# Two 64x128 transposes for four 64x64 ones, in a fused retention and MoE kernel

## The chip, the cores and the metric

The kernel runs on one core of a Trainium2 chip, in one launch. The metric is the device time of that launch in microseconds (us). The profile is one more execution, recorded by the hardware profiler; its span runs from the core's first instruction to its last.

TensorE (PE in the profile) multiplies and transposes, VectorE (DVE), ScalarE (ACT) and GpSimd (POOL) do the elementwise work, and SyncE (SP) issues most of the DMAs. A TensorE operation is two instructions: a weight load (PEld), which puts one operand into the array, and a matmul, which streams the other one through it. A transpose is such a pair, with the data as the loaded operand and an identity matrix as the streamed one. Each pair names a part of the array, a tile, by its rows and columns: 128x128 is the whole array, four 64x64 tiles can work side by side, and so can two tiles of 64 rows by 128 columns.

## The reference

A decaying, causal, unnormalised attention over 8 batches, 8 heads, 576 positions and a head size of 64 is followed by a feed-forward block on 4608 tokens with 512 features and 1024 hidden units:

```python
scores = scale * np.matmul(q, k.transpose(0, 1, 3, 2))
Dmat   = np.where(rel >= 0, gamma[:, None, None] ** rel[None, :, :], 0.0)
attn   = np.matmul(scores * Dmat[None], v)             # -> x, 4608 x 512
h      = x @ w_in
solu   = h * softmax(h)
ln     = (solu - mean(solu)) / sqrt(var(solu) + 1e-06) * g_ln
out    = ln @ w_out
```

All inputs and the output are float32.

## The kernel before

The sequences are cut into windows of 256 positions, with the four 64-position ends of four sequences put together as one more window. That makes 18 windows; each is worked as two *steps* `i` of four heads (36 steps) and gives two *tiles* `t` of 128 tokens to the feed-forward block (36 tiles). Within a step the heads go in two pairs, `hp` 0 and 1.

Per step, TensorE does these operations; the letters are those of the hand-written order in `ORDER["PE"]`:

- `T{i}` transposes the scaled q and k into a PSUM bank pair (`qk_tp`). For steps 0 to 11 it does so with whole-height transposes (line 360, tiles of 128x64), from step 12 on (`NQ = 12`) by the helper `turn` (line 307). ACT then copies the result out (`qe`, line 372).
- `J{i}` and `I{i}` multiply by the carried state (line 378). Between them, `Z{i}` is an empty instruction on SP (POOL for the first nine steps) that waits for `J{i}` and releases `I{i}`.
- `V{i}` (scores by v) and `K{i}` (the new state) are on line 378 too, `S{i}` (the scores) on line 422. All five use 64x64 tiles.

Per tile it does `M1_t` (line 502, 8 matmuls of 128x128 by 512 columns, x by w_in), `L{t}`, the transposes of the normalised hidden units (`ln_tp`: line 571, 128x128, for tiles 0 to 7; from tile 8 on, `NL = 8`, by `turn` on line 307), and `M2_t` (line 598, 8 matmuls by w_out). ACT copies `L`'s result out (`le`, line 582).

`turn(dst, src, odd)` transposes a block of 128 rows by 128 columns in quarters. `r` is the half of the rows and also the PSUM bank of the result; `e` is the half of the columns, which becomes the half of the partitions. With `odd` set (head pair `hp = 1`) the two halves of the partitions change places, which is the swap of the two heads. One call makes four transposes on the four 64x64 tiles. `T` calls it eight times, four times with `odd` and four times without, in the order q pair 0, q pair 1, k pair 0, k pair 1, two calls each. `L` calls it eight times, never with `odd`.

The order on each engine is written out in `ORDER`. A typical stretch on TensorE is

```python
"V20 K21 S21 M1_18 M2_16 L17 J21 T23 I21 V21 K22 S22 M1_19 M2_17 J22 L18 T24 I22 V22 K23 S23 "
```

A planner (`order_ops`) gives each operation a start time from `DUR` and from the instruction counts `COUNT`, with which it models how TensorE's instructions are fetched. These times interleave the engines' lists in the emitted program; within an engine the list is kept as it is. They also decide how many filler matmuls (`stir`, line 773) go into gaps before 31 us.

Of the kernel before, what the change touches and what calls it, by code (L numbers as in the profile page):

```python
# [16 lines left out]
    T=0.26, L=0.26, Tf=0.47, Lf=0.47, M1=1.73, M1a=1.3, M1b=0.44, M2=1.73, M2h=0.88, J=0.08, I=0.08, Z=0.05, S=0.23, V=0.225, K=0.13, G=0.1, WM=1.0, WS=0.95,  # L17
# [3 lines left out]
    ld=0.5, ld4=2.6, ldw=0.6, out=1.1, out4=2.2, outh=2.2, outz=1.1, lm=0.5,  # L21
)
MOVE = dict(ld=0.91, ld4=0.91, ldw=1.3, out=1.1, out4=1.1, outh=0.6, outz=0.6, lm=0.4)
COUNT = dict(T=64, L=64, Tf=32, Lf=16, S=32, V=32, K=32, J=8, I=8, G=2, WM=8, WS=2, M1a=12, M1b=4)
FETCH = ((20, 6.6), (45, 5.6), (999, 4.8))
PE_OUT = 0.2
SWITCH = 0.1
# [95 lines left out]
def order_ops(ops, caps):  # L123
# [27 lines left out]
    while len(start) < len(ops):  # L151
# [19 lines left out]
        if o.eng == "PE":  # L171
# [4 lines left out]
            mode = m  # L176
            fetched += COUNT.get(o.kind, 16)
            while fetched > ring:
# [52 lines left out]
def kernel(  # L231
# [10 lines left out]
    nc = tc.nc  # L242
    B, H, S, D = q.shape
# [28 lines left out]
    ident = const.tile([P, P], F16)  # L272
# [29 lines left out]
    ee = [slice(0, 64), slice(64, 128)]  # L302

    def turn(dst, src, odd=0):
        for r in range(2):
            for e in range(2):
                nc.tensor.transpose(  # L307
                    out=dst[ee[e ^ odd], r], in_=src[ee[r], e], identity=ident[ee[r], ee[r]]
                )

    def half(n):
        return ps["b"].rearrange("p r x -> p (r x)").bitcast(F16).rearrange(
            "p (r n q) -> p r n q", r=2, q=64)[:, :, 8 * n : 8 * n + 8]
# [33 lines left out]
    def flat(n):  # L347
        return ps["b"][:, n].bitcast(F16).rearrange("p (n q) -> p n q", q=P)

    def qk_tp(i):  # L350
        d = st[i]
        for n, src in enumerate((d["q16"], d["k16"])):
            for hp in range(2):
                for j in range(2):
                    x, pair = 4 * n + 2 * hp + j, src[:, j, 2 * hp : 2 * hp + 2]
                    if i >= NQ:
                        turn(half(0)[:, :, x], pair, hp)
                        continue
                    for e in range(2):
                        nc.tensor.transpose(out=flat(0)[ee[e ^ hp], x], in_=pair[:, e], identity=ident)  # L360
# [205 lines left out]
    def ln_tp(t):  # L566
        d = tk[t]
        for c in range(8):
            x = d["solu"][:, c * P : (c + 1) * P]
            if t < NL:  # L570
                nc.tensor.transpose(out=flat(1)[:, c], in_=x, identity=ident)  # L571
            else:
                turn(half(1)[:, :, c], x.rearrange("p (e q) -> p e q", e=2))

    def ln_ev(t):
        d = tk[t]
# [127 lines left out]
    for t in range(NT):  # L704
        w, c = divmod(t, 2)
# [15 lines left out]
        if c:  # L721
            op(f"q2{w}", "ACT", "q2", [f"ex{t}"], lambda w=w: squares(w))
            op(f"rs{w}", "POOL", "rs", [stat[t - 1], stat[t], f"q2{w}"], lambda w=w: rstd(w), [("sml", [f"oe{t}", f"oe{NT}" if t == NT - 1 else ""])])
        lb = "b"
        op(f"L{t}", "PE", "Lf" if t < NL else "L", [f"so{t}"], lambda t=t: ln_tp(t), [(x, [f"le{t}"]) for x in ("b2" if t < NL else "b1", "b3")], lb)
        op(f"le{t}", "ACT", "le", [f"L{t}"], lambda t=t: ln_ev(t), [("lnT", [f"M2_{t}", f"M2_{NT}" if t == NT - 1 else ""])], lb)
        for n in (t,) if t < NT - 1 else (t, NT):
# [9 lines left out]
    for c in range(4):  # L737
# [5 lines left out]
        out=masks, in_=nc.inline_tensor(masks_np, name="masks").ap().rearrange("p (m j) -> p m j", m=2)))  # L743
# [85 lines left out]
```

## Time and profile before

| | us |
|---|---|
| median of 3 runs | 223.62 |
| lowest and highest run | 223.28, 223.90 |
| the profiled execution's own time | 222.45 |
| its span | 220.7 |

| engine | busy us | share of the span |
|---|---|---|
| PE | 203.2 | 92% |
| PEld | 110.9 | 50% |
| DVE | 142.2 | 64% |
| ACT | 155.4 | 70% |
| POOL | 131.7 | 60% |

The mean granted TensorE clock was 0.988 of full speed. The profile's records give each matmul's start; its end is modelled, so neighbouring matmuls overlap in it and a "busy" PE says little. What a matmul costs is read from start to start. `turn` is first used at 66.0 us (`T12`) and last at 211.8 us (`L35`), with 1664 transposes: 896 from the hidden units, 384 from q and 384 from k.

### The profile page before, as it was taken

How to read it: one execution, taken by the hardware profiler on the slowest of the kernel's cores; microseconds unless marked ns; L12 is line 12 of the kernel's file. 1: busy time of each engine (PE TensorE's matmuls, PEld its weight loads, DVE VectorE, ACT ScalarE, POOL GpSimd, SP SyncE). 2: the span in 40 equal slices, each digit the busy share in tenths (PEclk: the TensorE clock that was granted, in tenths of full speed). 3: DMA queues.
4: the chain of work that ended last, by engine and by line, in shares of the span. 5: the costliest groups of instructions: out<-in, count | busy, mean ns of one | idle time of the engine just before them, and what ended most of it. 6: DMA issues, size and time to landing. Idle time of an engine off the chain costs nothing.

```text
span 220.7 us, 10333 instructions
## 1 busy us (share of the span) xinstructions
PE 203.2 (92%) x4468; PEld 110.9 (50%) x4468; DVE 142.2 (64%) x263; ACT 155.4 (70%) x303; POOL 131.7 (60%) x204
## 2 busy tenths in 40 slices
PE   7868988799999999999999999989999999999970
PEld 2434444564555555555555655545555555544440
DVE  1555579999659554765768586867667676566500
ACT  2356455478668786779697979777778878767950
POOL 2473719999886346597396967767697856001110
PEclk9996999999999999999999999999999999999998
DMA  6999999990796464779976766786863640261243
GB/s 180 304 353 341 345 323 287 279 291 19 210 266 160 113 156 106 215 222 289 324 215 205 223 200 195 228 253 176 246 189 88 146 120 6 51 147 38 61 111 83
DMA packets 65838, 42.83 MB, mean 194 GB/s; under 512 B 4088, under 2 KB 59776, under 8 KB 65792
## 3 DMA queue, kind: packets, MB, share of 16 engines
q1 hardware_dynamic: 65392, 42.02, 67.9%
q8 instruction: 35, 0.57, 1.2%
q10 hardware_dynamic: 400, 0.14, 0.3%
q14 instruction: 11, 0.09, 0.1%
HBM read 32.71 MB, written 9.44 MB: 191 GB/s over the span
## 4 chain that ended last, share of the span: by engine, by line
PE 71%; SPq 7%; DMA 7%; ACT 4%; DVE 3%; POOL 3%; issue 2%; POOLq 0%; DVEq 0%; ACTq 0%
PE score L598 25%; PE psh L502 25%; PE psx L378 7%; PE psb L307 6%; DMA qr<-in_q_dram 5%; SPq L321 3%; PE score L422 3%; DMA out_dram<-o_sb 2%; SPq L328 2%; DVE w2c L647 2%; SPq L620 1%; ACT o_sb L608 1%; PE psb L360 1%; PE psb L571 1%; PE psb L638 1%
## 5 line engine op out<-in xcount | busy, mean ns | idle before, releaser
L502 PE MATMUL psh<-w_in,xT 128*128 128x512 f16 x280 | 66.6, 380 | 2.3 <-DVE solu L534 1.5
L598 PE MATMUL score<-w2c,lnT 128*128 128x512 f16 (+1 forms) x288 | 66.6, 376 | 0.0
L520 ACT ACTIVATE e_sb<-psh 128x1024 f32<-128x1024 f32 x35 | 35.8, 1023 | 22.1 <-PE psh L502 22.0
L454 DVE TENSOR_TENSOR ret<-score,masks 128x512 f16<-128x512 f32 x72 | 46.2, 683 | 5.9 <-PE score L422 5.9
L598 PEld LDWEIGHTS <-lnT 128*128 128x128 f16 x296 | 28.6, 98 | 33.5 <-ACT lnT L582 1.0
L336 POOL TENSOR_TENSOR k<-kr,small 128x512 f16<-128x512 f32 x36 | 38.3, 1067 | 6.9 <-DMA kr<-in_k_dram 6.0
L502 PEld LDWEIGHTS <-xT 128*128 128x128 f16 x288 | 25.6, 98 | 31.4 <-issue 3.1
L336 POOL TENSOR_TENSOR q<-qr,small 128x512 f16<-128x512 f32 x34 | 36.2, 1068 | 7.9 <-DMA qr<-in_q_dram 7.9
L608 ACT ACTIVATE o_sb<-score,rs 128x512 f32<-128x512 f32 (+1 forms) x36 | 24.5, 681 | 14.6 <-PE score L598 6.8
L534 DVE TENSOR_TENSOR solu<-psh,e_sb 128x1024 f16<-128x1024 f32 x17 | 20.8, 1223 | 19.6 <-ACT e_sb L520 19.5
L480 POOL TENSOR_TENSOR g<-tt,small 128x128 f32<-128x128 f32 x32 | 13.3, 416 | 31.4 <-DVE tt L476 31.3
L529 DVE SCALAR_TENSOR_TENSOR solu<-psh,e_sb 128x1024 f16<-128x1024 f32 x18 | 22.0, 1224 | 9.2 <-ACT e_sb L520 9.2
L540 DVE BATCH_NORM_STATS2 bs<-solu 128x6 f32<-128x512 f16 x36 | 22.9, 679 | 0.1
L492 ACT CAST xT<-psx 128x512 f16<-128x512 f32 x36 | 21.2, 588 | 2.0 <-DVE g L471 1.3
L563 POOL TENSOR_TENSOR w<-q,mv 128x2 f32<-128x2 f32 x18 | 3.5, 195 | 29.8 <-ACT junk L549 16.9
L549 ACT ACTIVATE junk<-solu,s 128x1024 f16<-128x1024 f16 x18 | 20.7, 1149 | 0.6
L378 PE MATMUL psx<-qkT,s 64*64 64x128 f16 (+1 forms) x256 | 17.9, 228 | 2.3 <-SPq L410 1.3
L344 POOL CAST v<-vr 128x512 f16<-128x512 f32 x30 | 19.2, 641 | 0.0
L422 PE MATMUL score<-qkT 64*64 64x128 f16 x576 | 15.6, 221 | 2.4 <-ACT qkT L366 2.3
L582 ACT COPY lnT<-psb 128x512 f32<-128x512 f32 x28 | 16.4, 584 | 1.5 <-PE psb L307 0.8
L378 PEld LDWEIGHTS <-s 64*64 64x64 f16 x256 | 8.7, 105 | 14.6 <-issue 6.4
L378 PE MATMUL psx<-ret,v 64*64 64x128 f16 x576 | 15.9, 221 | 0.0
(64 smaller groups left out, 252.2 us busy)
## 6 DMA issues: line engine op xcount, KB each, us to landing
kr<-in_k_dram SPq DMA_DIRECT2D x32, 256.0 KB, 5.2
qr<-in_q_dram SPq DMA_DIRECT2D x32, 256.0 KB, 4.5
vr<-in_v_dram SPq DMA_DIRECT2D x32, 256.0 KB, 4.5
out_dram<-o_sb SPq DMA_DIRECT2D x64, 128.0 KB, 3.4
w_in_f<-in_moe_w_in_dram SPq DMA_DIRECT2D x4, 512.0 KB, 7.3
w_f<-in_moe_w_out_dram SPq DMA_DIRECT2D x4, 512.0 KB, 5.7
kr<-in_k_dram SPq DMA_DIRECT2D x16, 64.0 KB, 3.6
vr<-in_v_dram SPq DMA_DIRECT2D x16, 64.0 KB, 3.3
```

The costliest lines, as they stand in the source:

```text
L336: eng.tensor_tensor(out=t.rearrange("p j h d -> p h j d"), in0=st[i][nm + "r"], in1=g_of(i, base), op=ALU.mult,)
L378: m = nc.tensor.matmul(start=(c, e) not in begun, stop=False, skip_group_check=True, **kw)
L422: nc.tensor.matmul(out=sv[e][ee[c], hp, j], lhsT=qkT[ee[e], c, 1, hp, j], rhs=qkT[ee[e], c, 0, hp], start=True, stop=True,)
L454: nc.vector.tensor_tensor(out=d["ret"][:, e].rearrange("p h j q -> p h (j q)"), in0=score[e].rearrange("p (h x) -> p h x", h=2), in1=masks ...
L492: nc.scalar.copy(out=d["xT"].rearrange("p c h q -> p c (h q)"), in_=ps["x"][:, :, 0:256])
L502: nc.tensor.matmul(out=h_ps[:, half_], lhsT=st[2 * w + dc // 2]["xT"][:, c, dc % 2], rhs=w_in16[:, dc, 512 * half_ : 512 * half_ + 512], s ...
L520: nc.scalar.activation(out=d["e"], in_=hh(t), func=ACT.Exp, accum_out=ws[w]["se"][:, c : c + 1])
L529: nc.vector.scalar_tensor_tensor(out=d["solu"], in0=hh(t), scalar=1.0, in1=d["e"], op0=ALU.mult, op1=ALU.mult, accum_out=d["s1"][:, 0:1],)
L534: nc.vector.tensor_tensor(out=d["solu"], in0=hh(t), in1=d["e"], op=ALU.mult)
L540: nc.vector.bn_stats(out=bs[:, x], in_=tk[t]["solu"][:, x * 512 : x * 512 + 512])
L598: nc.tensor.matmul(out=o[:, cols], lhsT=tk[t]["lnT"][:, c].rearrange("p r q -> p (r q)"), rhs=w2c16[:, c, cols], start=(c == 0), stop=(c = ...
L608: nc.scalar.activation(out=d["osb"][:, cols], in_=o[:, cols], func=ACT.Copy, scale=ws[t // 2]["rs"][:, t % 2 : t % 2 + 1],)
```

## The change

Where there is no swap of heads, `turn` makes one transpose for each half of the rows: 64 rows by 128 columns go to all 128 partitions of the half's PSUM bank. With the swap it works as before. The planner's counts follow.

```diff
-COUNT = dict(T=64, L=64, Tf=32, Lf=16, ...
+COUNT = dict(T=48, L=32, Tf=32, Lf=16, ...
...
     def turn(dst, src, odd=0):
         for r in range(2):
+            if not odd:
+                nc.tensor.transpose(out=dst[:, r], in_=src[ee[r]], identity=ident[ee[r], ee[r]])
+                continue
             for e in range(2):
                 nc.tensor.transpose(
-                    out=dst[ee[e ^ odd], r], in_=src[ee[r], e], identity=ident[ee[r], ee[r]]
+                    out=dst[ee[1 - e], r], in_=src[ee[r], e], identity=ident[ee[r], ee[r]]
                 )
...
-                turn(half(1)[:, :, c], x.rearrange("p (e q) -> p e q", e=2))
+                turn(half(1)[:, :, c], x)
```

All of `L8` to `L35` and half of each of `T12` to `T35` change. The order of operations on every engine stays the same; on PE, 1280 transposes of 64x64 become 640 of 64x128.

More of the change, by code (lines that the diff above doesn't have):

```diff
@@ L23 @@
 MOVE = dict(ld=0.91, ld4=0.91, ldw=1.3, out=1.1, out4=1.1, outh=0.6, outz=0.6, lm=0.4)
-COUNT = dict(T=64, L=64, Tf=32, Lf=16, S=32, V=32, K=32, J=8, I=8, G=2, WM=8, WS=2, M1a=12, M1b=4)
+COUNT = dict(T=48, L=32, Tf=32, Lf=16, S=32, V=32, K=32, J=8, I=8, G=2, WM=8, WS=2, M1a=12, M1b=4)
 FETCH = ((20, 6.6), (45, 5.6), (999, 4.8))
```

## Prediction

> **What bounds the kernel now.** I read the page's engine shares and chain first.
>
> ```profile
> PE 203.2 (92%) x4468; PEld 110.9 (50%) x4468; DVE 142.2 (64%) x263; ACT 155.4 (70%) x303; POOL 131.7 (60%) x204
> PE 71%; SPq 7%; DMA 7%; ACT 4%; DVE 3%; POOL 3%; issue 2%; POOLq 0%; DVEq 0%; ACTq 0%
> ```
>
> TensorE carries 71% of the chain. As its busy time uses modelled ends, I then took the timeline of PE over one step (columns: start, length, engine, line, operation, tile rows*columns, streamed size, count):
>
> ```profile
> 122.30 1.90 PE L502 MATMUL psh<-w_in,xT 128*128 128x512 f16 x8
> 124.03 1.89 PE L598 MATMUL score<-w2c,lnT 128*128 128x512 f16 x8
> 125.85 0.45 PE L307 MATMUL psb<-ident,solu 64*64 64x64 f16 x32
> 126.13 0.23 PE L378 MATMUL psx<-qkT,s 64*64 64x128 f16 x4
> 126.19 0.29 PE L307 MATMUL psb<-ident,q 64*64 64x64 f16 x16
> 126.31 0.30 PE L307 MATMUL psb<-ident,k 64*64 64x64 f16 x16
> 126.47 0.25 PE L378 MATMUL psx<-qkT,s 64*64 64x128 f16 x4
> 126.55 0.39 PE L378 MATMUL psx<-ret,v 64*64 64x128 f16 x16
> 126.77 0.29 PE L378 MATMUL psx<-v,k 64*64 64x64 f16 x16
> 126.89 0.40 PE L422 MATMUL score<-qkT 64*64 64x128 f16 x16
> 127.22 0.39 PE L502 MATMUL psh<-w_in,xT 128*128 128x512 f16 x1
> ```
>
> From start to start, M1 takes 1.73 us, which is 8 times 0.216, and M2 starts with no gap. M2's eight would then end at 125.76, but L starts at 125.85: 0.09 us are lost where the tile goes from 128x128 to 64x64. Between L, J, T, I, V, K and S the line changes and the tile doesn't, and the single records put the usual gap there at 0 to 6 ns. From 66 to 206 us the starts leave only seven gaps over 0.3 us, 3.8 us together; the rest is a row of matmuls and these changes of tile. So in the stretch where `turn` is used, TensorE sets the pace, and ACT, the next, is busy 8.4 of 10 us there (the table by stage, 114 to 124 us).
>
> The question is then what a change of tile costs where only the rows or only the columns change. The early, whole-height T shows both (timeline, two windows):
>
> ```profile
> 46.66 0.25 PE L378 MATMUL psx<-qkT,s 64*64 64x128 f16 x4
> 46.84 0.41 PE L360 MATMUL psb<-ident,q 128*64 128x128 f16 x8
> 47.09 0.39 PE L360 MATMUL psb<-ident,k 128*64 128x128 f16 x8
> 47.41 0.25 PE L378 MATMUL psx<-qkT,s 64*64 64x128 f16 x4
> ...
> 49.22 0.41 PE L360 MATMUL psb<-ident,k 128*64 128x128 f16 x8 [0.15 <-POOL k L336]
> 49.57 0.62 PE L571 MATMUL psb<-ident,solu 128*128 128x128 f16 x8
> ```
>
> A group of concurrent matmuls with 128 columns streamed paces at 0.056 us (16 of `ret,v` on four tiles: 126.55 to 126.77). J's four from 46.66 should end at 46.72; T starts at 46.84, 0.12 late. T's k, four pairs from 47.09, should end at 47.31; the next starts at 47.41, 0.10 late. So a change of rows alone costs like a full one. In the second window only the columns change: k after a wait, from 49.22, takes four pairs of 0.056 and 0.02 more at its start and should end at 49.47; L starts at 49.57, 0.10 late. Taken from the single records, all changes without a visible wait lose 93 to 124 ns, and the second group after one comes another 10 ns (into 128x128) or 20 to 24 ns late (into 64x64 and 128x64).
>
> **The change part by part.**
>
> *Streaming.* 320 groups of four 64x64 transposes become 320 pairs of 64x128. A group now takes 31.5 ns (L: 8 groups in 0.28 us, less 0.02 for the first). A pair streams the same 64 columns, so half of the 56 ns for 128 columns, 28 ns, is the floor. Its weight load has 128 columns for 64. Loads by form:
>
> ```profile
> L598 PEld LDWEIGHTS <-lnT 128*128 128x128 f16 x296 | 28.6, 98 | 33.5 <-ACT lnT L582 1.0
> L307 PEld LDWEIGHTS <-solu 64*64 64x64 f16 x896 | 9.9, 108 | 5.1 <-issue 4.7 <-DVE bs L540 0.4
> ```
>
> A 128-column load is no longer than a 64-column one (98 against 108 ns), but no row has it on half the rows. Ends: 28 ns (320 x -3.5 = -1.1 us) and 56 ns, the pace of the 128x128 transposes of line 571, should the load of 128 columns set it (320 x 24.5 = +7.8). I take 30 ns, near the load row: -0.5 us.
>
> *Changes of tile.* `turn` without `odd` now stands on 64x128 between operations on 64x64. T runs q pair 0 (64x128), q pair 1 (64x64), k pair 0, k pair 1: three changes inside each of 24 T, 72. The others come where L and T begin and end. Counted along TensorE's order in the two programs there are 118 changes before and 231 after: 113 more, of which 48 lead into 64x64 and 65 into 64x128. Into 64x64 a change costs 93 + 22 = 0.116 us by the rows: 48 x 0.116 = 5.6. Into 64x128 the nearest rows are those that leave 64x64 with one dimension grown (64x64 to 128x64, 100 to 124 ns, plus 24) and that go to 128 columns (99 plus 10): I take 0.12, and 65 x 0.12 = 7.8. Together +13.4 us. Ends: 113 x 0.093 = 10.5 and 113 x 0.142 = 16.0; the pair 64x64 and 64x128 itself stands in no row, so that it costs nothing stays open as a rival. Queued behind each of these are V, K, S, M1 and M2 of the same step, so the loss goes straight to the next step; ACT and DVE, who wait for T and L, have slack.
>
> The Trainium skill (TensorEngine Tiling (Array Packing), Key Properties) says that a change of tiling mode drains TensorE, and a change of tile within a mode does not. The rows agree for each pair of shapes they hold. By the rule all 113 drain; without it for this pair the sum would be that of the first rival.
>
> *Fewer instructions.* 640 loads and 640 matmuls go. The Trainium skill (TensorE: Matmul & The Clock Gate, "Wait — 56ns, not 53.3ns?") has matmul starts never closer than some 25 ns; by that 640 fewer would save an estimated 16 us. The rows speak against it: 32 transposes of L start within 0.28 us, under 9 ns apart. So the saving is that of the streaming term.
>
> *Stalls that go.* Of the 3.8 us of gaps, four (0.37, 0.71, 0.58, 0.36) are I waiting for Z on SP, which stands behind DMA issues:
>
> ```profile
> 162.62 0.11 PEld L378 LDWEIGHTS <-s 64*64 64x64 f16 x4 [0.63 <-SPq L410]
> ```
>
> T lies between J and I; with some 0.4 us more in it, and SP's work unchanged while the step grows, I take 1.6 of these 2.0 us as covered. Two more (0.95 in M1 at 147 us, 0.53 in T at 106 us) show no releaser but "issue"; instructions arrive by DMA (the page's instruction queue: 35 packets, 0.57 MB, so 16 KB each), and with a seventh fewer I take 0.8 of 1.5 us as gone. Sum -2.4; ends 0 and -3.5. What comes next late is TensorE itself.
>
> Early work (up to 66 us) is untouched: T0 to T11 and L0 to L7 use other lines. Loads are issued ahead and only wait longer for buffers.
>
> *Sum:* +13.4 - 0.5 - 2.4 = +10.5 us. The profiled execution took 222.45 us (span 220.7 and 1.75 around it), which gives 232.95; it lies 1.2 under the median of the runs, so against 223.62 I forecast 234.1 us. All low ends: 10.5 - 1.1 - 3.5 = +5.9, 229.5 us. High ends without slow loads: 16.0 - 0.5 + 0 = +15.5, 239.1.
>
> **The rivals.**
>
> *Half-row tiles don't drain among themselves (faster).* If 64x64 and 64x128 count as one shape, the 113 changes cost nothing. Then -0.5 to -1.1 of streaming and about -0.8 of issue gaps remain: 222.0 us. This decides when a change between the two costs below some 12 ns (1.3 / 113). For it: both split the rows in the same way, and no row shows the pair. Against it: a change of columns alone cost 0.10 us, three times out of three.
>
> *Slow loads.* If a load of 128 columns on 64 rows sets the pace, pairs take 56 ns: +7.8 instead of -0.5, so 242.4 us. For it: no load on half the rows with 128 columns is in the trace. Against: the 98 ns row.
>
> *The drains are partly hidden.* If they cost half, because the next load may go to the other half of the rows early, or because other stalls shrink more, then about +13.4 / 2 - 0.5 - 2.4 = +3.8: 227.4 us. Against: from 64x64 tiles, where the same could happen, rows show the full price.
>
> **How the numbers follow.** Full drains with quick loads 0.70 (229.5 to 239.1, likeliest 234.1); slow loads 0.16; partly hidden 0.07; no drain 0.06; no visible change 0.01. The likeliest gives 234.1. Leaving out no drain, most of the partly hidden case and the upper part of slow loads, the range is 229.0 to 242.5. About 0.3% (0.7 us) is what a measurement of this kernel can tell from no change. Faster by more: 0.06; within: 0.02; slower: 0.92.
>
> **What would show it.** In the profile after, T's four parts should start some 0.17 to 0.19 us apart (two pairs or groups and a change) where q and k now take 0.12 each, so that T takes 0.65 to 0.75 us in place of 0.28; J should start about 0.12 us later after L; a step of 4.92 us should become 5.4 to 5.5. L's 16 transposes should start some 15 ns apart; at 28 ns the loads are slow. The SP waits of I should be mostly gone. I am wrong if T's parts follow one another without a gap, if the steps stay below 5.1 us, or if the step grows and the end doesn't.

## The result and the profile after

| | before | after |
|---|---|---|
| median us | 223.76 (4 runs) | 230.31 (4 runs, 228.82 to 231.2) |
| ratio, 95% interval | | 1.0293 [1.0223, 1.0363] |
| the profiled execution, its span | 222.45, 220.7 | 230.1, 228.3 |

The changed kernel is 2.9% slower, some 6.5 us. One of the four runs of before (228.05 us) was in a slower state; the ratio is taken without it. The page of the changed kernel, engine shares and chain by engine:

```profile
PE 213.6 (94%) x3828; PEld 116.1 (51%) x3828; DVE 142.1 (62%) x263; ACT 155.3 (68%) x303; POOL 131.4 (58%) x204
PE 80%; SPq 5%; ACT 4%; DMA 3%; DVE 2%; POOL 1%; issue 1%; POOLq 0%; DVEq 0%; ACTq 0%
```

There are 640 matmuls fewer, and TensorE has 80% of the chain in place of 71%; the other engines do what they did. One step on the timeline of PE (columns as before; line 307 is now the 64x128 transpose of `turn` and line 310 its 64x64 one, and the numbers below them are three higher):

```profile
150.19 1.89 PE L601 MATMUL score<-w2c,lnT 128*128 128x512 f16 x8
152.01 0.41 PE L307 MATMUL psb<-ident,solu 64*128 64x64 f16 x16
152.35 0.25 PE L381 MATMUL psx<-qkT,s 64*64 64x128 f16 x4
152.53 0.23 PE L307 MATMUL psb<-ident,q 64*128 64x64 f16 x4
152.69 0.26 PE L310 MATMUL psb<-ident,q 64*64 64x64 f16 x8
152.88 0.23 PE L307 MATMUL psb<-ident,k 64*128 64x64 f16 x4
153.04 0.26 PE L310 MATMUL psb<-ident,k 64*64 64x64 f16 x8
153.13 0.23 PE L381 MATMUL psx<-qkT,s 64*64 64x128 f16 x4
153.19 0.39 PE L381 MATMUL psx<-ret,v 64*64 64x128 f16 x16
153.41 0.29 PE L381 MATMUL psx<-v,k 64*64 64x64 f16 x16
153.53 0.40 PE L425 MATMUL score<-qkT 64*64 64x128 f16 x16
153.86 1.90 PE L505 MATMUL psh<-w_in,xT 128*128 128x512 f16 x8
```

T's four parts start 0.16 to 0.19 us apart, though each streams only two groups (0.06 us). T takes 0.60 us, from 152.53 to 153.13, where it took 0.28. J comes 0.34 us after L's start and not 0.28, although L's 16 transposes are as quick as its 32 were: by the single records they start 14.7 ns apart, a pair every 29.3 ns. The loads are no longer:

```profile
L307 PEld LDWEIGHTS <-solu 64*128 64x128 f16 x448 | 8.1, 95 | 6.0 <-issue 4.7 <-DVE bs L543 0.4
L310 PEld LDWEIGHTS <-q 64*64 64x64 f16 x192 | 3.5, 104 | 1.2
```

128 columns on half the rows take 95 ns, 64 columns 104. The Trainium skill (TensorE: Matmul & The Clock Gate, "Weight-path perf modes — Fast Weight Load (FWL) and DoubleRow") has loads of exactly 128 columns that are not FP32 go by a faster path; the two rows agree with that.

To see where the time went, I sorted each start-to-start interval of TensorE, from T12's first transpose to the end, in one profiled execution of each kernel. The pace of a group (31.5 ns for four 64x64 with 64 columns, 29.2 for a pair, 56 for 128 columns, 216 for 512) counts as streaming. What the first group after a change of tile comes late (to 130 ns) and the next one (to 26 ns) counts as changes; lateness over 140 ns elsewhere, or over those limits, counts as stalls. What is left is small lateness. The time after the start of the last matmul is the tail.

| us | before | after | difference |
|---|---|---|---|
| changes of tile (65, then 177 in this stretch) | 7.27 | 20.11 | +12.84 |
| transposes of `turn`, streaming | 13.04 | 12.36 | -0.68 |
| all other streaming and small lateness | 123.36 | 121.49 | -1.87 |
| stalls | 4.88 | 1.31 | -3.57 |
| after the last matmul's start (tail) | 6.07 | 5.26 | -0.81 |
| sum, from T12 on | 154.62 | 160.53 | +5.91 |
| ahead of T12 | 66.04 | 67.79 | +1.75 |

The last row isn't the change: nothing differs there, and over the eleven profiles that this document has, T12 starts anywhere from 66.0 to 68.7 us. The profile of before happens to be an early one.

### The profile page after: what moved, and what is told of

Read it like the earlier page. It is cut to its first block, busy times and chain, and to the rows that moved or that the text cites. A ratio compares the mean times of both kernels' runs of the same rounds, so it can differ in the third digit from the quotient of the medians.

```text
span 228.3 us, 9053 instructions
## 1 busy us (share of the span) xinstructions
PE 213.6 (94%) x3828; PEld 116.1 (51%) x3828; DVE 142.1 (62%) x263; ACT 155.3 (68%) x303; POOL 131.4 (58%) x204
## 4 chain that ended last, share of the span: by engine, by line
PE 80%; SPq 5%; ACT 4%; DMA 3%; DVE 2%; POOL 1%; issue 1%; POOLq 0%; DVEq 0%; ACTq 0%
PE psh L505 27%; PE score L601 26%; PE psx L381 8%; PE psb L307 7%; PE psb L310 4%; SPq L324 3%; PE score L425 3%; DMA qr<-in_q_dram 3%; PE psb L574 2%; PE psb L363 2%; DVE w2c L650 2%; SPq L331 1%; ACT qkT L369 1%; PE psb L641 1%; PE psx L505 1%
## 5 line engine op out<-in xcount | busy, mean ns | idle before, releaser
L457 DVE TENSOR_TENSOR ret<-score,masks 128x512 f16<-128x512 f32 x72 | 46.2, 682 | 7.6 <-PE score L425 7.6
L474 DVE TENSOR_TENSOR g<-psx,g 128x128 f32<-128x128 f32 x16 | 4.6, 290 | 17.4 <-PE psx L381 17.4
```

The source lines that it names most:

```text
L457: nc.vector.tensor_tensor(out=d["ret"][:, e].rearrange("p h j q -> p h (j q)"), in0=score[e].rearrange("p (h x) -> p h x", h=2), in1=masks ...
```

## The experiments

The theory after the result: a change of tile idles TensorE for 0.115 us, whichever dimension changes, and the sum of them, less what TensorE had been waiting for anyway, is the loss. The rivals: the 64x128 transposes themselves are slow; added work in T costs more than its length; the loss goes with the number of wide transposes.

### Spare transposes in the kernel before

```diff
+    def wide(dst, src):
+        for r in range(2):
+            nc.tensor.transpose(out=dst[:, r], in_=src[ee[r]], identity=ident[ee[r], ee[r]])
...
                     if i >= NQ:
+                        if j == 0 and (n, hp) == (1, 0):
+                            wide(half(0)[:, :, x], pair)
                         turn(half(0)[:, :, x], pair, hp)
```

The second cut is in `qk_tp`, which makes T. One spare 64x128 call for each T: 

> The kernel before, with one more call in each of T12 to T35: before k's first call, the same block is transposed once as two 64x128 pairs (its result is then written again by the 64x64 ones). 48 changes of tile and 24 pairs more, nothing else moved. Theory (each change of tile idles TensorE for about 0.115 us, and TensorE sets the pace): 24 x (0.114 + 0.116 + 0.03) = 6.2 us more TensorE time, of which up to 3.8 us of stalls may give back: 226.5 to 229.8 us. Rival (the changes are free, the wide transposes themselves or their loads are slow): 24 pairs at 0.056 us, +1.3 us or less: 224 to 225 us.

Measured: 227.01 us, ratio 1.0132 [1.0076, 1.0188]. The timeline of PE shows the one call (line 313 is `wide`, line 384 was 378):

```profile
151.36 0.29 PE L307 MATMUL psb<-ident,q 64*64 64x64 f16 x16
151.59 0.20 PE L313 MATMUL psb<-ident,k 64*128 64x64 f16 x2
151.72 0.32 PE L307 MATMUL psb<-ident,k 64*64 64x64 f16 x16
151.87 0.23 PE L384 MATMUL psx<-qkT,s 64*64 64x128 f16 x4
```

k starts 0.36 us after q, where it started 0.12 after it, for two transposes put in. By the accounting the changes cost 5.60 us more, 0.117 each, and the stretch from T12 on grew by 3.32. Of the 6.3 us put in (0.7 of it streaming) 3.0 came back: 1.1 of small lateness, 0.4 of stalls and 1.45 of the tail.

The same call as four 64x64 transposes (against that run):

```diff
                         if j == 0 and (n, hp) == (1, 0):
-                            wide(half(0)[:, :, x], pair)
+                            turn(half(0)[:, :, x], pair)
```

> The control of the run with a spare 64x128 call: the same spare call in the same place of T12 to T35, but as four 64x64 transposes, so no change of tile is added. Theory: 24 x 0.0315 = 0.8 us of TensorE, 223.5 to 224.8 us. Rival (any added work there costs like the wide call): 226.5 us or more.

Measured: 223.84 us against 223.65, ratio 1.0012 [0.9966, 1.0059]. The same work in the same place without a change of tile is not seen in the time. This pair separates the change of tile from the work.

Three spare 64x128 calls, ahead of every part of T but the first (against the run with one):

```diff
-                        if j == 0 and (n, hp) == (1, 0):
+                        if j == 0 and (n, hp) != (0, 0):
                             wide(half(0)[:, :, x], pair)
```

> The kernel before, with three spare 64x128 calls in each of T12 to T35 (before q pair 1, k pair 0 and k pair 1): 144 changes of tile more. Theory: 72 x 0.26 = 18.7 us more TensorE time; the stalls can be given back only once, so from one spare call to three the time should grow by the full 48 x 0.26 = 12.5 us: 238 to 242.5 us. Rival (the time that goes back grows with the added time, because much of TensorE's time is cover for something else): less than 10 us above the run with one spare call.

Measured: 238.23 us, ratio 1.0621 [1.054, 1.0703], 11.2 above one call. The changes cost 16.54 us more than before, 0.115 each, so the price is the same with 48, 112 (the change itself) and 144 more of them. Of the 12.3 us between one call and three (10.9 of changes, 1.4 of streaming) 2.4 came back as stalls: the expectation had assumed that one call would take all stalls away, and it had not.

### Half of the change

Here `turn` takes a fourth argument, and makes the 64x128 transposes only where it is 1. L alone on 64x128 (against the changed kernel):

```diff
-COUNT = dict(T=48, L=32,
+COUNT = dict(T=64, L=32,
...
-                        turn(half(0)[:, :, x], pair, hp)
+                        turn(half(0)[:, :, x], pair, hp, 0)
```

> Only L uses the 64x128 transposes, T stays on 64x64 (in the kernel before's order of operations): 158 changes of tile against 118, 40 more, 896 fewer instructions. Theory (changes of tile): 12 x 0.116 + 28 x 0.12 = 4.8 us more, 0.8 us less streaming, 1 to 3.5 us of stalls given back: 224.5 to 227 us. Rival (L, with 448 of the 640 wide transposes, brings most of the loss, because the wide transposes are slow): 228 us or more.

Measured: 223.64 us, ratio 1.0 [0.9958, 1.0041], below the theory's range. 448 of the 640 wide transposes cost nothing visible. The 40 changes cost 4.51 us, and all came back: streaming -0.46, other -1.14, stalls -1.93 and the tail -1.32. The tail's share is partly scatter: the 6.07 us in the profile of before is the longest of all, and the others have 4.6 to 5.4.

T alone on 64x128 (against the changed kernel too):

```diff
-COUNT = dict(T=48, L=32,
+COUNT = dict(T=48, L=64,
...
-                turn(half(1)[:, :, c], x)
+                turn(half(1)[:, :, c], x.rearrange("p (e q) -> p e q", e=2), 0, 0)
```

> Only T uses the 64x128 transposes, L stays on 64x64: 213 changes of tile, 95 more, though only 192 of the 640 wide transposes are in it. Theory: 47 x 0.116 + 48 x 0.114 = 10.9 us more, 0.4 less streaming, 2 to 3.5 of stalls given back: 230 to 232.5 us, no better than the whole change. Rival (loss by the number of wide transposes): 226 us or less.

Measured: 227.95 us, ratio 1.0193 [1.0132, 1.0254]. Below the range again, but 4.3 us above L alone, with 192 wide transposes against 448 and 95 changes against 40. The loss goes with the number of changes, not with that of wide transposes. The theory's error is once more the part that comes back: changes +10.73, stalls -2.72, other -1.28.

### The same transposes in another order

```diff
-        for n, src in enumerate((d["q16"], d["k16"])):
-            for hp in range(2):
+        for hp in range(2):
+            for n, src in enumerate((d["q16"], d["k16"])):
                 for j in range(2):
```

In the changed kernel this puts the 64x128 parts of q and k side by side: 

> The changed kernel with T's parts in the order q pair 0, k pair 0, q pair 1, k pair 1: the same transposes, but one change of tile inside T and not three, 48 changes fewer (183 in the program). Theory: 48 x 0.115 = 5.5 us less TensorE time than the changed kernel, of which 0.5 to 2 us may come back as stalls: 225 to 227 us. Rival (the wide transposes or their loads cost the time): no change against the changed kernel, 229 to 231 us.

Measured: 224.81 us, ratio to before 1.0024 [0.998, 1.0067]. By the medians, swapping two loops takes back some 5.5 us of the 6.5, with all 640 wide transposes in place:

```profile
149.74 0.23 PE L307 MATMUL psb<-ident,q 64*128 64x64 f16 x4
149.81 0.22 PE L307 MATMUL psb<-ident,k 64*128 64x64 f16 x4
149.96 0.26 PE L310 MATMUL psb<-ident,q 64*64 64x64 f16 x8
150.04 0.23 PE L310 MATMUL psb<-ident,k 64*64 64x64 f16 x8
150.11 0.23 PE L381 MATMUL psx<-qkT,s 64*64 64x128 f16 x4
```

q and k of one shape start 0.07 to 0.08 us apart, and only the step between the shapes takes 0.15. This kernel still has 64 changes more than before from T12 on (129 and 65), yet its stretch from T12 to the end is only 0.81 us longer (155.43 and 154.62 us): what came back covers nearly all of them.

One step further, T is split in two operations, U (pair 0 of q and k) and T (pair 1), and the order is rewritten (one step as an example):

```diff
-        "L17 J21 T23 I21 V21 K22 S22 M1_19 M2_17 J22 L18 T24 I22 "
+        "L17 U23 J21 T23 I21 V21 K22 S22 M1_19 M2_17 L18 U24 J22 T24 I22 "
```

> The changed kernel with the 64x128 work of a step in one piece: L, then q pair 0 and k pair 0, then J, then q pair 1 and k pair 1, then I (where L can go first). 152 changes of tile, 34 more than before, 32 of them into 64x128, and all 1280 instructions fewer. Theory: 32 x 0.11 + 2 x 0.116 = 3.7 us more than before, 0.7 less streaming, 1.5 to 2.5 less by gaps in which instructions are late, 0 to 3 us more of I waiting for Z, since only half of T lies between J and I now: 223.5 to 227 us. Rival (loss by wide transposes, not by changes): as the changed kernel, 229 to 231 us.

Measured: 225.06 us, ratio 1.0064 [1.0024, 1.0103]. Changes were +3.39 us only, but stalls rose to 5.90 from 4.88: with half of T between J and I, I waits for Z in nearly every step, and most of these stalls are some 0.15 us each. What the order saved in changes it paid in an exposed wait.

L alone on 64x128 and moved to stand right behind M1 or M2 (against the run with L alone):

```diff
-        "M1_19 M2_17 J22 L18 T24 I22 V22 "
+        "M1_19 M2_17 L18 J22 T24 I22 V22 "
```

> Only L on 64x128, T on 64x64, and L moved to stand right behind M1 or M2 in each step, so that it takes one change more and not two: 143 changes, 25 more than before, 896 fewer instructions. Theory: 28 x 0.105 - 3 x 0.116 = 2.6 us more, 0.8 less streaming, 1 to 2 less by gaps in which instructions are late; L may wait for VectorE, which it reaches earlier: 222.5 to 225.5 us, level with the kernel before. Rival (L's earlier place exposes VectorE's product in each step, 0.2 us or more): 227 us or more.

Measured: 224.04 us, ratio 1.0017 [0.9982, 1.0053]: changes +2.29, stalls +0.21. It is level with L alone in the old order: that one has 15 more changes (2.2 us) and 2.1 us less of stalls, five of its gaps and eight here being I waiting for Z. None of these versions beats the kernel before.

### What the gaps without a releaser come from

In the profile of before, TensorE's waits from 69 to 208 us, then those of the run with a spare 64x64 call (columns: who waited for whom, us, times, longest):

```profile
PE psx L378 <- SPq L410: 1.3, 4, 0.5
PE psh L502 <- issue: 0.8, 1, 0.8
PE psb L307 <- issue: 0.3, 1, 0.3
```
```profile
PE psh L504 <- issue: 1.1, 1, 1.1
PE psx L380 <- SPq L412: 1.1, 2, 0.9
PE score L424 <- issue: 0.9, 1, 0.9
```

"Issue" gaps without any semaphore appear in four programs: before, both one-call runs and three calls, which have 8936 TensorE instructions or more. The change and its variants, with 7656 to 8552, have none. One such gap lies in the middle of M1, between its second matmul and its third (timeline of PE in before):

```profile
146.87 0.60 PE L502 MATMUL psh<-w_in,xT 128*128 128x512 f16 x2
148.26 0.38 PE L502 MATMUL psh<-w_in,xT 128*128 128x512 f16 x1 [0.79 <-issue]
```

So the changed kernel was given its number of instructions back, each wide pair being made twice:

```diff
-        for r in range(2):
+        for r in (0, 1) if odd else (0, 1, 0, 1):
             if not odd:
```

> The changed kernel with each 64x128 pair of transposes made twice in a row: as many TensorE instructions as in the kernel before again, the 231 changes of tile of the changed kernel, and 320 pairs more. Streaming: 320 x 0.0293 = 9.4 us. Theory one (the gaps of TensorE without a releaser, 1 to 2.4 us in the programs with 8900 instructions or more and none in those with up to 8500, come with the number of instructions): they are back, 1 to 2.4 us in one to three gaps, and the time is 240.5 to 242.5 us. Theory two (they went because the steps grew longer, or with the shape of the transposes): no such gap, 239 to 240 us.

Measured: 238.44 us, ratio 1.0693 [1.0597, 1.0789], and no such gap: the number alone isn't it, and the time lies below both ranges, 8.1 us above the change for 9.3 of streaming. What sorts the programs is how fast they use instructions up. Over the steps from 100 to 185 us, TensorE's records (weight loads and matmuls) per us are

| before, spare 64x64 | one spare call | three | twice | T alone | L alone, L first | grouped, joined | after |
|---|---|---|---|---|---|---|---|
| 52.6 | 51.3 | 49.0 | 47.1 | 46.8 | 46.2, 45.8 | 42.4 to 42.5 | 41.0 |
| gaps | gaps | one gap | none | none | none | none | none |

The first three columns have gaps (1.06 to 2.4 us in all), the others none.

The traces show more. Number TensorE's loads and matmuls in the order of their starts. All seven "issue" gaps between 69 and 210 us end at number 190 or some multiple of 256 beyond it, and each program has as many 16 KB packets in its instruction queue (35 in before, 30 in the changed kernel) as it has such places. Pair the second place with the first packet, the third with the second, and so on: in all eleven traces no place is passed less than 1.37 us after its packet landed. The instruction behind each of the seven gaps starts 1.37 to 1.53 us after the landing, and in the seven programs without gaps every place between 69 and 210 us has at least 1.67 us. By this the gaps are waits for the next block of 256 instructions. That a program falls behind because it uses instructions up too fast fits the table, but no run changed the rate by itself.

## Why the prediction was right or wrong

The direction and the mechanism held, and the time, 230.31, lies in the range, but only 1.3 us inside its low end. The forecast of +10.5 us was 4 too high. Point by point:

- *Changes of tile*: +13.4 forecast, +12.84 measured, 0.115 each (93 + 22 ns in the forecast is 0.115 too, not 0.116, which is 0.05 us in its sum). The pair that no row of before held costs 93 to 95 ns plus 20 to 24 into 64x64, and from 64x64 into 64x128 102 to 128 plus 9 to 11. The rival in which half-row tiles don't drain among themselves is out, and with it the partly hidden drains. The rule of the Trainium skill (TensorEngine Tiling (Array Packing), Key Properties) holds for this pair too.
- *Streaming*: 30 ns a pair forecast, 29.3 measured; -0.5 against -0.68. The slow loads are out (95 ns).
- *Stalls that go*: this term was mis-sized. I counted the gaps over 0.3 us, 3.8, and let 2.4 go; 3.57 went, nearly all. Of the gaps of I waiting for Z some 1.8 went (1.6 forecast), of the two issue gaps all 1.5 (0.8 forecast), and 0.3 ahead of S that had no place in the sum. Beside them 1.87 us went that I had not counted at all: lateness of a few ns to 0.1 us each, mostly within T's and L's 64x64 groups and on both sides of I. In the kernel before, each of q's groups behind the first comes 5 ns late on the mean, in the changed kernel none does. It isn't the new shape alone that does this: with one or three spare wide calls, where all 64x64 groups stay, the small lateness falls by some 1.1 to 1.2 us as well, and with the spare 64x64 call by 0.1. Together 5.4 us came back and not 2.4.
- *The sum*: 12.84 - 0.68 - 5.44 - 0.81 (the tail, whose scatter I had not allowed for) = 5.91 us from T12 on, in place of 13.4 - 0.5 - 2.4 = 10.5. The runs' 6.5 us are 0.6 more; one profile of each kernel can't say where these lie.
- *What would show it*: T's parts 0.16 to 0.19 us apart (0.17 to 0.19 forecast), T 0.60 (0.65 to 0.75), J some 0.06 later (0.12), a step of 5.30 us here (M1 at 153.86 and again at 159.16) and 5.40 at the median of those from 100 to 185 us (5.4 to 5.5). All as expected or a little under.

## What to carry to other kernels

Where TensorE sets the pace, count the places where the tile's shape changes along its order, not the instructions: here each cost 0.115 us of TensorE's time, as much as some 15 of the 64x64 transposes. When a shape is worth having for part of the work, put that work side by side; swapping two loops was worth some 5.5 us. And when time is added to an engine, read all of its lateness first, the small intervals too, because the new time fills it before it shows at the end: L alone put in 4.5 us of changes and its time stayed that of the kernel before.

## What was not expected of the hardware

The price of a change of tile doesn't depend on how much changes: only the columns (64x128 and 64x64), only the rows (64x64 and 128x64) and both (64x64 and 128x128) all lose 92 to 128 ns. And a dense row of small tiles can wait for its own instructions: in the programs that used 49 or more of them per us, gaps of 0.3 to 1.3 us without a releaser stood where a new block of 256 begins, and at 47.1 or fewer there was none.
